# Attention, a greedy router and eight experts in one kernel: the router's and the experts' instructions put in order by one list scheduler, and the second pieces of the weights computed on VectorE

## The chip, the cores and the metric

The kernel runs on one core of a Trainium2 chip. The core has TensorE (PE, matrix products into the accumulator memory PSUM), VectorE (DVE), ScalarE (ACT), GpSimd (POOL), SyncE (SP) and DMA queues. Each engine works through its own queue in order, and the engines wait for each other by semaphores. The metric is the device time of one execution in microseconds (us).

## What is computed

Causal attention with a bias over 8 batches, 8 heads, 576 positions and 64 channels gives 4608 tokens of 512 channels. A router assigns the tokens to 8 experts, and each expert is a two-layer network:

```python
attn = softmax(where(causal, scale * q @ k.T + min(bias, 0), -1e9))
x = (attn @ v).transpose(0, 2, 1, 3).reshape(4608, 512)
logits = x @ w_gate                                # 8 experts
for idx in argsort(-logits.flatten()):             # greedy, from the largest logit on
    tok, e = idx // 8, idx % 8
    if assigned[tok] < 0 and counts[e] < 576:      # 576 places in each expert
        assigned[tok] = e; counts[e] += 1
for e in range(8):
    m = assigned == e
    out[m] = maximum(x[m] @ w1[e], 0) @ w2[e]      # 512 -> 1024 -> 512
```

## The kernel before

**Pieces.** Products are made of 16-bit pieces: an operand is split into a first piece (rounded to f16) and a second one (the remainder), and three of the four products of pieces are summed in PSUM. So every weight of an expert is loaded in f32 into a buffer `wst` and split. An expert has 12 loads: 4 of `w1` (128x1024, 512 KB) and 8 of `w2` (128x512, 256 KB), gathered by an indirect DMA on GpSimd's queue (L1012), since the router decides which expert comes next.

**The split before.** `Moe.weights` makes the first piece on ScalarE (L1017). For most loads ScalarE then scales the buffer in place (L1019) and GpSimd subtracts (L1027). For some loads of `w1` (three of expert 0's, the third of the others') one VectorE instruction over 1024 columns does both (L1025).

**The attention** comes first and keeps an order of its own. Only its comments differ between the two kernels.

**The router** (`Router`) fills one expert per phase, eight phases. A phase looks for the threshold at which some expert's remaining places are used up: seven steps, one digit each. In a step VectorE compares all keys with 32 digits (`ge`, L820), TensorE counts (L834), VectorE copies (`ca`, L838), TensorE sums (L844), VectorE compares with the places left (`pe`, L846), TensorE spreads this (L851), and VectorE takes the digit (`jc`, L854), subtracts (`wd`, L857) and goes on. Each link waits for the one before. `choose` (L773 to L788) prepares a phase; the update of the unassigned tokens (L921 to L937) ends it. `places` (L944 to L980) turns the chosen tokens into ids: one-hot matrices `ob`, `rv`, `ol` on VectorE, 40 small products on TensorE (`pi`, L973, in two groups of 20), then `ids`.

**The experts.** With the ids of an expert GpSimd gathers its tokens (`xg`, L1042), five tiles of 128 (the last of 64). SyncE transposes them by DMA into `xT`; for expert 0 TensorE does (L1052). The first layer is 8 groups of 12 pairs of products (512 columns in L1075, 64 in L1076), each followed by a ReLU on ScalarE (L1080) and a remainder on VectorE (L1089). The second layer is 112 products of 512 columns (L1109, L1100); ScalarE scales the result and GpSimd scatters it (L1121).

**The order.** `Clock` holds a rough time for each engine. A loop walks through the products of expert after expert, and after each product lets the search, the places and the loads go on when their time by a table (`AFTER`, `PACE`, `LAT` and others) has come, the router at most two phases ahead. Constant products (`warm`, L1251: 10, 16 and 12 of them) stand in the wait before expert 0.

Of the kernel before, what the change touches and what calls it, by code (L numbers as in the profile page):

```python
# [18 lines left out]
S = 576  # L19
# [7 lines left out]
QS = 32.0                 # scale of the q and k pieces  # L27
YS = 8.0 * QS * QS        # scale of the exponents in PSUM
# [22 lines left out]
class Attention:  # L51
# [23 lines left out]
    # ---- constants  # L75
# [27 lines left out]
    def gate(self):  # L103
        """The gate's pieces."""
# [85 lines left out]
    def prep_units(self, g):  # L190
        """Pieces of q, k, v. Pass 1 is [q hi; aux] . [k hi; aux], pass 2 is [q hi; q lo] . [k lo; k hi]."""
# [63 lines left out]
    def q0(self, par, i):  # L255
        """Where query tile i of a head lies: an odd head's last 64 queries come first."""
# [74 lines left out]
    def st_units(self, g):  # L331
        """S^T, exp, remainder of one group; returns units."""
# [145 lines left out]
    def tail(self, g, pr):  # L478
        """The last batch, two heads at a time, with transposes on the tensor engine: a list of units."""
# [71 lines left out]
    def run(self):  # L551
# [10 lines left out]
        def later(n0, units):  # L562
            """A list of (step, unit), made when step n0 comes."""
# [93 lines left out]
WARM = (10, 16, (2, 2, 2, 2, 4))  # L657
YSC = 1.0 / (VS * WS1 * WS2)
# what the order of the instructions goes by (us)
RLATE = 0.3  # L660
SLATE = -1.0
PACE = 1.7
GPACE = 1.8
PLEAD = 0.7
LAT = 3.3
HOP = -0.6
AHEAD = 0.5
DV0 = (0, 1, 2)
DV = (2,)
EARLY = 4  # L670
EARLY2 = 1
WARM = (10, 16, (2, 2, 2, 2, 4))
YSC = 1.0 / (VS * WS1 * WS2)
MARGIN = (0.0, 0.2)
# [8 lines left out]
class Router:  # L683
# [73 lines left out]
    def psum(self, shape, dt=F32):  # L757
        return self.ps.tile(shape, dt, name="psr")
# [601 lines left out]
```

## Time and profile before

| | |
|---|---|
| device time, median of 3 runs (lowest to highest) | 919.23 us (917.11 to 926.0) |
| span of the profiled execution | 923.2 us |
| TensorE busy, share of the span | 811.1 us, 88% |
| weight loads on TensorE | 484.3 us, 52% |
| VectorE | 656.4 us, 71% |
| GpSimd | 550.6 us, 60% |
| ScalarE | 460.6 us, 50% |
| read from and written to the chip's memory | 72.49 and 19.49 MB |

A span is the time from the first to the last instruction of the profiled execution; it lies 4.0 us above the median of the runs. A busy share is an average over very different stages: attention fills the first 399 us, the search for the first expert some 44 more, and the rest belongs to experts and router together. TensorE is the busiest engine, but its busy time holds products at a reduced clock too. Rows of the trace give a start and a length in us, the engine, the line of the kernel, the operation, the output and the inputs, and in brackets how long the engine had been idle before and what it waited for.

### The profile page before, as it was taken

Reading aid. Unit: us, or ns where it says so; the run is one execution under the profiler, and the core shown is the slowest. Engines: PE = TensorE matmul, PEld = TensorE weight load, DVE = VectorE, ACT = ScalarE, POOL = GpSimd, SP = SyncE. Lnnn points to the kernel's source line nnn. Section 1 sums busy time; section 2 is a strip of 40 time slices with the busy share of each in tenths; the row PEclk is TensorE's granted clock in tenths of the full one; section 3 lists DMA queues with packets and bytes.
Section 4 is the critical chain, followed back from the end, with each engine's and each line's share of the span. In section 5 each row is a group of like instructions: output and inputs, shape, how many; then the busy total and the mean of one; then the engine's idle time right before and its main releaser. Section 6 shows DMA issues by size and latency. Waiting matters only on the chain.

```text
span 923.2 us, 22391 instructions
## 1 busy us (share of the span) xinstructions
PE 811.1 (88%) x8719; PEld 484.3 (52%) x8719; DVE 656.4 (71%) x2077; ACT 460.6 (50%) x952; POOL 550.6 (60%) x582
## 2 busy tenths in 40 slices
PE   2889999989998999946998769989899989899996
PEld 0456676757676777723543334444444545444442
DVE  6895898989898987877887496896868874413010
ACT  5465676667775767713541352543524343526411
POOL 5544565656674677605646666686766675767601
PEclk9995798979897999966998799999999999999999
DMA  7763685978876772414324536446484537547201
GB/s 191 230 162 110 173 201 138 184 190 207 195 212 170 185 186 45 111 53 143 82 102 122 113 126 139 156 104 151 138 132 151 133 118 178 122 123 178 91 13 40
DMA packets 118400, 129.17 MB, mean 140 GB/s; under 512 B 79889, under 2 KB 80405, under 8 KB 118294
## 3 DMA queue, kind: packets, MB, share of 16 engines
q1 hardware_dynamic: 100114, 74.81, 34.6%
q0 software_dynamic: 15744, 52.46, 19.1%
q8 instruction: 68, 1.11, 0.5%
q10 hardware_dynamic: 2436, 0.48, 0.3%
q14 instruction: 38, 0.31, 0.1%
HBM read 72.49 MB, written 19.49 MB: 100 GB/s over the span
## 4 chain that ended last, share of the span: by engine, by line
PE 47%; DVE 23%; issue 11%; POOL 8%; DMA 7%; ACT 2%; SPq 0%; POOLq 0%; ACTq 0%; DVEq 0%
PE py L1109 9%; PE ph L1075 6%; PE po L408 5%; PE pst L339 5%; PE pst L341 4%; PE pss L275 4%; DMA wst<-in_w_dram,iw 3%; PE po L410 3%; PE po L409 3%; DVE scr L269 2%; DVE ge L820 2%; POOL wst L1012 2%; PE pst L344 2%; PE pss L288 2%; POOL xg L1042 2%
## 5 line engine op out<-in xcount | busy, mean ns | idle before, releaser
L351 POOL TENSOR_TENSOR R<-P 128x512 f16<-128x512 f32 x158 | 179.6, 1144 | 119.5 <-ACT P L349 57.0
L1075 PE MATMUL ph<-xT,w1p 128*128 128x512 f16 x768 | 205.3, 392 | 4.2 <-DMA xT<-xg 4.2
L1109 PE MATMUL py<-w2p,hT 128*128 128x512 f16 x768 | 180.4, 386 | 0.0
L349 ACT ACTIVATE P<-pst 128x512 f32<-128x512 f32 (+1 forms) x224 | 122.5, 553 | 98.8 <-PE pst L344 67.3
L1076 PE MATMUL pht<-xT,w1p 128*128 128x64 f16 x768 | 150.4, 196 | 1.9 <-DMA xT<-xg 1.9
L269 DVE CUSTOM_DVE_ANT_0 scr<-pss,mS 128x512 bf16<-128x512 f32 (+3 forms) x256 | 120.5, 482 | 32.3 <-PE pss L275 21.9
L1012 POOL DMA_INDIRECT wst<-in_w_dram,iw x96 | 98.8, 1030 | 66.0 <-issue 26.6
L408 PE MATMUL po<-V,P 128*128 128x65 f16 (+1 forms) x960 | 136.1, 206 | 0.1
L410 PE MATMUL po<-V,R 128*128 128x65 f16 (+1 forms) x960 | 134.0, 202 | 2.2 <-DVE R L351 2.2
L339 PE MATMUL pst<-Q,K 70*128 70x384 f16 (+4 forms) x576 | 133.3, 265 | 2.4 <-ACT P L349 2.4
L409 PE MATMUL po<-Vl,P 128*128 128x64 f16 (+1 forms) x960 | 134.0, 201 | 0.0
L341 PE MATMUL pst<-Q,K 128*128 128x384 f16 (+4 forms) x576 | 132.1, 262 | 0.0
L1075 PEld LDWEIGHTS <-w1p 128*128 128x128 f16 x768 | 76.7, 100 | 96.1 <-issue 17.0
L1109 PEld LDWEIGHTS <-hT 128*128 128x128 f16 x768 | 70.5, 99 | 80.0 <-issue 5.5
L408 PEld LDWEIGHTS <-P 128*128 128x128 bf16 (+1 forms) x960 | 95.2, 103 | 22.5 <-issue 9.5
L409 PEld LDWEIGHTS <-P 128*128 128x128 bf16 (+1 forms) x960 | 97.3, 106 | 5.1 <-issue 3.0
L410 PEld LDWEIGHTS <-R 128*128 128x128 f16 (+1 forms) x960 | 97.6, 104 | 2.3 <-DVE R L351 2.3
L275 PE MATMUL pss<-K,Q 67*128 67x512 f16 (+3 forms) x256 | 78.3, 342 | 21.5 <-DMA K<-pk 13.0
L1080 ACT ACTIVATE hT<-ph 128x512 f16<-128x512 f32 x64 | 37.8, 592 | 112.8 <-PE ph L1075 85.8
L1027 POOL TENSOR_TENSOR w2p<-wst,w2p 128x512 f16<-128x512 f32 x64 | 75.9, 1190 | 26.2 <-ACT wst L1019 25.4
L1121 POOL DMA_INDIRECT out_dram<-y,ids x40 | 41.7, 1043 | 71.5 <-ACT y L1111 58.7
L1089 DVE SCALAR_TENSOR_TENSOR hT<-ph,hT 128x512 f16<-128x512 f32 x64 | 43.8, 686 | 53.0 <-ACT hT L1080 52.9
(215 smaller groups left out, 1683.3 us busy)
## 6 DMA issues: line engine op xcount, KB each, us to landing
rq<-in_q_dram SPq DMA_DIRECT2D x32, 288.0 KB
rk<-in_k_dram SPq DMA_DIRECT2D x32, 288.0 KB
rv<-in_v_dram SPq DMA_DIRECT2D x32, 288.0 KB
Q<-Q SPq DMA_DIRECT2D x62, 144.0 KB
K<-K SPq DMA_DIRECT2D x62, 144.0 KB
xs<-xp SPq DMA_DIRECT2D x32, 256.0 KB
wst<-in_w_dram,iw POOLq DMA_INDIRECT x96, 4.1
xs<-xp SPq DMA_DIRECT2D x8, 128.0 KB
```

The lines of the kernel that those rows point to most:

```text
L269: nc.vector.tensor_tensor_reduce(scr[:, :n], ps, mask, 1.0, init, OP.add, OP.max, o)
L339: nc.tensor.matmul(ps[o, c0:c0 + n], K[0:70, 0, par, pr, ks], Q[0:70, 0, par, pr, q0:q0 + n], start=True, stop=False)
L341: nc.tensor.matmul(ps[o, c0:c0 + n], K[:, 1, par, pr, ks], Q[:, 1, par, pr, q0:q0 + n], start=False, stop=not diag)
L349: nc.scalar.activation(P[:, c0:c0 + n], ps[:, :n], AF.Exp, scale=1.0 / YS)
L351: self.post(lambda: eng.tensor_tensor(R[:, c0:c0 + n], P[:, c0:c0 + n], strided_hi(P)[:, c0:c0 + n], op=OP.subtract), T["RT"][0 if gp else 1])
L408: nc.tensor.matmul(po[:n, i, :], H[rows, c:c + n], V[rows, pr, sl, :], start=f, stop=False)
L409: nc.tensor.matmul(po[:n, i, 0:64], H[rows, c:c + n], Vl[rows, pr, sl, :], start=False, stop=False)
L410: nc.tensor.matmul(po[:n, i, :], R[rows, c:c + n], V[rows, pr, sl, :], start=False, stop=l)
L1012: nc.gpsimd.indirect_dma_start(out=t[:, :n], out_offset=None, in_=src, in_offset=bass.IndirectOffsetOnAxis(ap=iw[:, k:k + 1], axis=0))
L1075: nc.tensor.matmul(ph, w, xT[:, 0:4, 4 * b + c], start=first, stop=last)
L1076: nc.tensor.matmul(pt[:, f], w, xT[:, 4, 4 * b + c, 0:64], start=first, stop=last)
L1109: nc.tensor.matmul(py, hT[:, f, a, 128 * i:128 * i + n], w2p[:, f, b], start=first, stop=last)
```

## The change

Search, places, loads, splits, gathers and products all become tasks of one graph (`Plan`). A task has an engine, a duration, the tasks it depends on, a priority and the buffers that it takes or uses; buffers come from rings with a fixed number of tiles. The list scheduler keeps a time for each engine and starts, again and again, the task that can start first; among those of an engine that are ready it takes the one of the best priority (router 0, remainders of the ReLU and gathers 1, an expert's loads, splits and products 2 + its number). A low task can be held back by 0.35 or 0.4 us if a better one comes soon. Router products have a `slack` of 0, 0.15 or 0.3 us (phase 0, 1, later). A load is taken to land 2.6 us after 1 us of issue and its share of a common 180 KB/us. The order in which tasks are started is the order of the instructions.

With it: every second piece of a weight is made by VectorE, in parts of 512 columns (L1221), two for a `w1` load; the scaling in place on ScalarE and the subtraction on GpSimd are gone. There are 5 `wst` buffers, not 4. Marking who reached a threshold (`jm`, `t`, `run`) is done once for six steps and once for the last, not in every step. The 40 place products form one group. The first three groups of expert 0's first layer come tile by tile, 128 columns each, as the tiles arrive. There are 16 constant products. Loads of `w2` of experts 0 and 1 wait for the ids.

```diff
+class Plan:
+    HOP = 0.04
+    KBUS = 180.0
...
+    def add(self, e, dur, f, deps=(), prio=1, takes=(), uses=(), lat=None, hold=0.0, kb=0, slack=0.0):
...
+        if e == "t":
+            x.occ, x.lat = dur, dur + 0.19
+        else:
+            x.occ = max(dur - dict(v=0.08, a=0.11, p=0.04, s=0.0)[e], 0.03)
+            x.lat = dur + self.HOP
...
+    def run(self):
+        while self.count:
+            best = None
+            for e, w in self.wait.items():
...
+                for t, x in sorted(c, key=lambda z: (z[1].prio, z[1].rank)):
+                    if t <= t0 + 1e-9:
+                        pick = (t, x)
+                        break
+                t, x = pick
+                if x.hold:
+                    soon = [z for z in c if z[1].prio < x.prio and z[0] < t + x.hold]
...
+            t, x = best
+            self.start(t, x)
...
+        x.at = t
+        if x.kb:
+            self.dma = max(self.dma, t + 1.0) + x.kb / self.KBUS
+            x.lat += self.dma - t
+        x.end = t + x.lat
+        self.free[x.e] = t + x.occ
...
-                yield AFTER["ca"]
-                pb = self.psum([128, E])
+                T(0.28, f_pa, takes=[A], uses=[ge])
+                V(0.19, lambda ca=ca, A=A, n=n: v.tensor_copy(
+                    ca.t[:4 * n], A.t[:4 * n, 0:32].rearrange("p (c e) -> p c e", c=4)), takes=[ca], uses=[A])
...
-            def hi():
-                t = box[0]
-                nc.scalar.activation(dst[:, 0], t[:, :n], AF.Copy, scale=sc)
-                if not ve:
-                    nc.scalar.activation(t[:, :n], t[:, :n], AF.Copy, scale=sc)
-                return n / 1200 * (1 if ve else 2)
-
-            def lo():
-                t = box[0]
-                if ve:
-                    nc.vector.scalar_tensor_tensor(dst[:, 1], t[:, :n], sc, dst[:, 0], op0=OP.mult, op1=OP.subtract)
-                    return "v", n / 900
-                nc.gpsimd.tensor_sub(dst[:, 1], t[:, :n], dst[:, 0])
-                return "p", n / 480
+            ld = pl.add("p", 1.0, lambda: nc.gpsimd.indirect_dma_start(
+                out=st.t[:, :n], out_offset=None, in_=src,
+                in_offset=bass.IndirectOffsetOnAxis(ap=iw.t[:, k:k + 1], axis=0)), [tw] + ([ti] if k >= 4 and j < 2 else []), prio=prio, takes=[st], uses=[iw],
+                lat=self.LAND, kb=n / 2)
+            first = key == 0
+            hi = pl.add("a", 1.05 if n == FF else 0.63, lambda: nc.scalar.activation(
+                dst.t[:, key, 0], st.t[:, :n], AF.Copy, scale=sc), [ld], prio=prio,
+                takes=[dst] if first else (), uses=[st] + ([] if first else [dst]), hold=0.4)
+            lo = [pl.add("v", 0.7, lambda c=c: nc.vector.scalar_tensor_tensor(
+                dst.t[:, key, 1, c:c + 512], st.t[:, c:c + 512], sc, dst.t[:, key, 0, c:c + 512], op0=OP.mult,
+                op1=OP.subtract), [hi], prio=prio, uses=[st, dst], hold=0.35) for c in range(0, n, 512)]
...
+    pl = Plan()
+    last = behind = None
+    for j in range(E):
+        info = {}
+        last = R.phase(pl, j, info, last, 0)
+        first = info if j == 0 else first
+        behind = M.expert(pl, j, info, behind, R.ident16 if j == 0 else None)
...
+    for n in range(16):
+        x = pl.add("t", 0.43, warm, [x], prio=1.5, uses=[hot])
+    pl.run()
```

What this does to the queues is seen at three places. In the tables a row is one instruction: line, operation, output<-inputs, size.

VectorE inside a router step, while an expert's products run. Before:

```order
L838 CAST ca<-psr 128x32
L861 TENSOR_SCALAR jm<-jc 128x1
L862 SCALAR_TENSOR_TENSOR t_10860<-psr,jm,Ws 128x8
L846 TENSOR_TENSOR pe<-psr,rem 128x8
L864 TENSOR_TENSOR run<-run,t_10860 128x8
L854 TENSOR_REDUCE jc<-psr 128x1
L857 TENSOR_SCALAR wd<-y,jc 128x40
L820 TENSOR_TENSOR ge<-wd,kj 128x1280
```

VectorE inside such a step in the changed kernel (`w1p` is the split weight):

```order
L1002 CAST ca_8801<-psa 128x32
L1221 SCALAR_TENSOR_TENSOR w1p_8859<-wst_8867,w1p_8859 128x512
L1010 TENSOR_TENSOR pe_8803<-psb,rem 128x8
L1221 SCALAR_TENSOR_TENSOR w1p_8859<-wst_8867,w1p_8859 128x512
L1015 TENSOR_REDUCE jc_8808<-psb 128x1
L1019 TENSOR_SCALAR wd_8806<-y_8799,jc_8808 128x40
L975 TENSOR_TENSOR ge_8798<-wd_8806,kj 128x1280
L986 SCALAR_TENSOR_TENSOR y_8800<-wd_8806,dg 128x40
L1221 SCALAR_TENSOR_TENSOR w1p_8859<-wst_8863,w1p_8859 128x512
```

The marking has left the step, and parts of second pieces stand where VectorE waits for TensorE's counts and sums.

GpSimd at the end of an expert, with the next one's loads and gathers. Before:

```order
L1012 DMA wst<-in_w_dram,iw 128x1024 x4
L1027 TENSOR_TENSOR w1p<-wst,w1p 128x1024
L1012 DMA wst<-in_w_dram,iw 128x512
L1027 TENSOR_TENSOR w1p<-wst,w1p 128x1024
L1012 DMA wst<-in_w_dram,iw 128x512
L1027 TENSOR_TENSOR w1p<-wst,w1p 128x1024
L1027 TENSOR_TENSOR w2p<-wst,w2p 128x512
L1012 DMA wst<-in_w_dram,iw 128x512
L1042 DMA xg<-xs,ids 128x1024
```

GpSimd at a like place in the changed kernel:

```order
L1213 DMA wst_8867<-in_w_dram,iw_8831 128x1024
L1213 DMA wst_8863<-in_w_dram,iw_8831 128x1024
L1213 DMA wst_8864<-in_w_dram,iw_8831 128x1024
L1187 DMA xg_8868<-xs,ids_8840 128x1024 x4
L1187 DMA xg_8868<-xs,ids_8840 64x1024
L1213 DMA wst_8865<-in_w_dram,iw_8831 128x1024
L1213 DMA wst_8866<-in_w_dram,iw_8831 128x512
L1213 DMA wst_8867<-in_w_dram,iw_8831 128x512
L1302 MEMSET spacer 1x1
L1303 DMA out_dram<-y_8875,ids_8839 4608x512
```

GpSimd's queue holds only the issue of transfers now, and the five gathers follow each other.

VectorE after the first search, on the way to expert 0's ids. Before:

```order
L944 SCALAR_TENSOR_TENSOR Z<-Y,X 128x80
L946 SCALAR_TENSOR_TENSOR si<-Z 128x40
L948 TENSOR_SCALAR d<-si 128x40
L949 TENSOR_SCALAR d<-si 128x40
L951 CAST db<-d 128x80
L958 TENSOR_TENSOR ob<-i_468,db 128x720
L961 TENSOR_TENSOR rv<-ob,rb 128x720
```

The same place in the changed kernel:

```order
L1119 SCALAR_TENSOR_TENSOR Z_8842<-Y_8835,X_8832 128x80
L1085 TENSOR_TENSOR tm_8819<-oh,gg_8813 128x320
L1120 SCALAR_TENSOR_TENSOR si_8843<-Z_8842 128x40
L1090 TENSOR_REDUCE cp_8820<-tm_8819 128x8
L1121 TENSOR_SCALAR d_8844<-si_8843 128x40
L1094 TENSOR_SCALAR sel_8822<-W,vstar_8826 128x8
L1122 TENSOR_SCALAR d_8844<-si_8843 128x40
L1095 TENSOR_TENSOR gv_8815<-gg_8813,U 128x40
L1123 CAST db_8845<-d_8844 128x80
L1096 TENSOR_SCALAR sel_8822<-sel_8822 128x8
L1127 TENSOR_TENSOR ob_8846<-i_468,db_8845 128x720
```

The update of the unassigned tokens (`tm`, `cp`, `sel` and what follows) has moved from behind the ids to between the steps that lead to them.

More of the change, by code (lines that the diff above doesn't have):

```diff
@@ L678, with __init__, slot @@
 NEG = -1.0e30
+SLACK = (0.0, 0.15, 0.3)
 NONE = 1.0e9
 NT = 8 * S
+class Buf:
+    __slots__ = ("ring", "t", "users")
+    def __init__(self, ring):
+        self.ring, self.t, self.users = ring, None, []
+class Ring:
+    def __init__(self, tiles):
+        self.slots = [[t, None] for t in tiles]
+    def slot(self):
+        best = None
+        for s in self.slots:
+            if s[1] is None:
+                at = 0.0
+            elif all(u.at is not None for u in s[1].users):
+                at = max(u.end for u in s[1].users)
+            else:
+                continue
+            if best is None or at < best[0]:
+                best = (at, s)
+        return best
@@ L985 @@
+        info["ids"] = (chain[0], ids)
 class Moe:
+    LAND = 2.6
     def __init__(self, tc, ctx, xs, w1, w2, out):
@@ new lines, in expert, with scatter, go @@
+        w2n = {(f, b): [W2[f][0]] if b == 0 else W2[f][1] for f in range(8) for b in range(2)}
+        def scatter(i, n, dep):
+            def go():
+                nc.gpsimd.memset(self.spacer, 0.0)
+                st = nc.gpsimd.indirect_dma_start(
+                    out=self.out, out_offset=bass.IndirectOffsetOnAxis(ap=ids.t[:n, i:i + 1], axis=0),
+                    in_=y.t[:n, i], in_offset=None)
+                for s in self.scat:
+                    self.tc.declare_no_dep(st.ins, s.ins, reason="other rows")
+                self.scat.append(st)
+            pl.add("p", 1.1, go, [dep], prio=2, uses=[y, ids], lat=3.0, kb=2 * n)
@@ L1170, in route_and_experts @@
+        return closing
 def route_and_experts(tc, ctx, R, xs, w1, w2, out):
     R.pools(ctx)
+    R.rings()
     M = Moe(tc, ctx, xs, w1, w2, out)
-    info = {j: {} for j in range(E + 1)}
-    clock = Clock()
-    now = dict(j=0, out=0)
-    def search():
-        for j in range(E):
-            yield from R.phase(j, lambda k, t, j=j: info[j].update({k: t}))
-    def places():
-        for j in range(E):
-            while "places" not in info[j]:
-                yield None
-            yield from R.places(j, *info[j]["places"], lambda k, t, j=j: info[j].update({k: t}))
@@ L1188, in route_and_experts @@
-    streams = [dict(g=g, next=0.0, ready=0.0, pe=0.0) for g in (search(), places())]
-    def step(s, force=False):
-        if clock.t < s["next"] and not force:
-            return False
-        clock.at["t"] = max(clock.t, s["ready"]) + s["pe"]
-        s.update(ready=0.0, pe=0.0)
-        x = next(s["g"], None)
-        if x is None:
-            return False
-        done = clock.use("v", x[0])
-        if x[1] is None:
-            s["next"] = done - AHEAD
-        else:
-            lead = sum("ids" in info[i] for i in range(E)) - now["j"]
-            s.update(next=done + x[1] + MARGIN[min(lead, 2) - 1], ready=done + HOP, pe=x[2])
-        return True
@@ L1208, in load @@
-    def load(j, k):
-        u = info[j]["wu"][k]
-        def hi():
-            clock.after("a", u[1](), 0.1, lo)
-        def lo():
-            clock.use(*u[2]())
-            now["out"] -= 1
-            info[j]["left"].discard(k)
-        u[0]()
-        now["out"] += 1
-        clock.after("p", 1.04, LAT, hi)
-    def fetch(j, force=False):
-        d = info[j]
-        if "weights" in d and "w1p" not in d:
-            d["w1p"], d["w2p"], d["wu"] = M.weights(d["weights"], dve=DV)
-            d["left"], d["next"] = set(range(12)), 0
-        if "ids" in d and "xT" not in d:
-            d["xT"], d["xu"] = M.gather(d["ids"])
-        if d.get("xu"):
-            clock.use("p", 1.04)
-            d["xu"].pop(0)()
-            return GPACE
-        if "wu" in d and d["next"] < 12 and (now["out"] < 4 or force):
-            while now["out"] >= 4:
-                clock.wait()
-            load(j, d["next"])
-            d["next"] += 1
-            return PACE
-        return None
@@ L1244, in route_and_experts @@
-    hot = []
-    def warm(n):
-        for _ in range(n):
-            if not hot:
-                hot.append(R.ps.tile([128, 512], F32, name="warm", tag="psr"))
-            tc.nc.tensor.matmul(hot[0], R.ones, R.qb.rearrange("p c n -> p (c n)"), start=True, stop=True)
-    d = info[0]
-    while "weights" not in d:
-        step(streams[0], True)
-    d["w1p"], d["w2p"], d["wu"] = M.weights(d["weights"], dve=DV0)
-    d["left"], d["next"] = set(range(4, 12)), 4
-    for u in d["wu"][:4]:
-        u[0]()
```

794 lines of the change are left out of this document (424 added, 370 removed).

## The prediction

> **What bounds the kernel now.** I first read the span and then the busy times by stretch, from the experts' first product (442.8, its row stands with the pace below) to their last (915.2): this stretch, the end behind it, the part in which the router still works, and a piece of that.
>
> ```profile
> span 923.2 us, 22391 instructions
> ...
> 442.80:915.20 472.40, 431.20 (x3361) 215.21 (x3356) 282.35 (x821) 190.05 (x289) 292.70 (x295) 0.96 0.47 121
> 915.20:923.20 8.00, 0.00 (x0) 0.00 (x0) 0.00 (x0) 0.48 (x1) 0.97 (x1) 0.71 0.08 33
> ...
> 442.80:800.00 357.20, 316.15 (x2647) 160.02 (x2643) 264.28 (x794) 148.48 (x224) 235.32 (x229) 0.94 0.51 130
> ...
> 680.00:740.00 60.00, 58.71 (x520) 30.39 (x519) 46.77 (x159) 23.11 (x36) 38.39 (x38) 1.00 0.67 148
> ```
>
> The numbers in a row are stretch, length, then busy us of PE, weight load, VectorE (DVE), ScalarE (ACT), GpSimd (POOL), and the granted clock. The expert stretch is bound by TensorE, which idles 472.4 - 431.2 = 41.2 us and runs at 0.96 of its clock; 0.04 x 472.4 = 18.9 us more go to that. So about 60 us could be had, and 431.2 - 18.9 = 412 us is the work. The pace of the products says the same:
>
> ```profile
> 442.78 0.38 PE L1075 MATMUL ph<-xT,w1p 128*128 128x512 f16 x1
> ...
> 540.50 0.38 PE L1075 MATMUL ph<-xT,w1p 128*128 128x512 f16 x1
> ...
> 544.66 0.38 PE L1075 MATMUL ph<-xT,w1p 128*128 128x512 f16 x1
> ...
> 909.70 5.34 PE L1109 MATMUL py<-w2p,hT 128*128 128x512 f16 x24
> ```
>
> From 540.50 to 544.66 seventeen steps of 0.245 us lie between the starts of the first layer's pairs, and 24 products of the second take (5.34 - 0.38) / 23 = 0.216 each. An expert has 96 pairs and 112 products: 96 x 0.245 + 112 x 0.216 = 47.7 us, eight of them 381.5. The other 30 us are the router's products, some 4.4 per expert: an expert needs 52 us of TensorE. I take 411 us for the whole.
>
> Then I asked which TensorE groups had waited, in the expert stretch (last part of a row: idle us before, and what ended it):
>
> ```profile
> L1075 PE MATMUL ph<-xT,w1p 128*128 128x512 f16 x768 | 205.3, 392 | 4.2 <-DMA xT<-xg 4.2
> L1076 PE MATMUL pht<-xT,w1p 128*128 128x64 f16 x768 | 150.4, 196 | 1.9 <-DMA xT<-xg 1.9
> L834 PE MATMUL psr<-oh,ge 128*128 128x32 f16 (+1 forms) x416 | 17.1, 177 | 9.9 <-DVE ge L820 9.8
> L973 PE MATMUL pi<-rv,ol 128*32 128x36 bf16 x280 | 12.4, 202 | 21.5 <-DVE ol L968 21.5
> L844 PE MATMUL psr<-ca,qb 128*128 128x8 f16 (+1 forms) x168 | 10.4, 167 | 2.7 <-DVE jm L861 2.7
> ```
>
> Of 41.2 us idle, 9.9 + 21.5 + 2.7 = 34.1 are router products that stand in TensorE's queue before VectorE has their operands; only 6.1 are a late transfer. Why VectorE is late, the chain of waits and GpSimd's timeline show for the longest of these waits:
>
> ```profile
> 541.47 2.33 DVE rv L961
> ...
> 544.11 2.71 DVE sel L929
> ...
> 547.58 3.77 DVE U L934
> ...
> 551.88 0.90 PE pi L973 x20
> ...
> 541.25 2.14 POOL L1027 TENSOR_TENSOR w1p<-wst,w1p 128x1024 f16<-128x1024 f32 x1
> ...
> 544.65 2.13 POOL L1027 TENSOR_TENSOR w1p<-wst,w1p 128x1024 f16<-128x1024 f32 x1
> ...
> 548.04 2.13 POOL L1027 TENSOR_TENSOR w1p<-wst,w1p 128x1024 f16<-128x1024 f32 x1
> 550.12 1.16 POOL L1027 TENSOR_TENSOR w2p<-wst,w2p 128x512 f16<-128x512 f32 x1
> ...
> L934 DVE TENSOR_TENSOR U<-U,X x7: 193/195/3842, 435.2 to 768.0; 128x40 f32<-128x40 f32 x7
> ...
> L934 DVE TENSOR_TENSOR U<-U,X 128x40 f32<-128x40 f32 x6 | 8.7, 1448 | 0.0
> ...
> 552.71 0.61 PE L1075 MATMUL ph<-xT,w1p 128*128 128x512 f16 x1
> ...
> 553.18 0.61 PE L1075 MATMUL ph<-xT,w1p 128*128 128x512 f16 x1
> ```
>
> Each long VectorE instruction ends when a GpSimd subtraction ends (543.8, 546.8, 551.3). The update of U takes 0.195 us at the median and 3.84 at worst (min/median/max in ns), and 1.448 on average over the experts' stretch; the chain that TensorE waits for was blocked three times in 10 us. Behind the wait pairs start 0.47 apart in place of 0.245: the clock is down.
>
> **The change part by part.** First, the second pieces leave GpSimd and ScalarE for VectorE.
>
> ```profile
> L1027 POOL TENSOR_TENSOR w2p<-wst,w2p 128x512 f16<-128x512 f32 x64 | 75.9, 1190 | 26.2 <-ACT wst L1019 25.4
> L1027 POOL TENSOR_TENSOR w1p<-wst,w1p 128x1024 f16<-128x1024 f32 x21 | 45.4, 2162 | 17.6 <-ACT wst L1019 17.4
> ...
> L1019 ACT ACTIVATE wst<-wst 128x512 f32<-128x512 f32 (+1 forms) x85 | 62.5, 735 | 7.5 <-ACT w2p L1017 0.4
> ...
> L1025 DVE SCALAR_TENSOR_TENSOR w1p<-wst,w1p 128x1024 f16<-128x1024 f32 x7 | 16.6, 2378 | 2.5 <-ACT w1p L1017 2.5
> ...
> L1025 DVE SCALAR_TENSOR_TENSOR w1p<-wst,w1p x10: 1211/1226/3742, 428.5 to 841.2; 128x1024 f16<-128x1024 f32 x10
> ...
> L1089 DVE SCALAR_TENSOR_TENSOR hT<-ph,hT 128x512 f16<-128x512 f32 x64 | 43.8, 686 | 53.0 <-ACT hT L1080 52.9
> ```
>
> GpSimd loses 121 us, ScalarE 62.5; neither bounds anything, so this alone is worth nothing. VectorE gets 8 x 16 = 128 parts of 512. One costs between half of 1.226 and the 0.686 of a like instruction on 512: I take 0.68, together 87 us, and 10 x 1.23 = 12 go. What it loses is the blocking. Its lower end is two groups alone: L934, 6 x (1.448 - 0.195), and L1025, 7 x (2.378 - 1.226), some 16 us. Its upper end is all of GpSimd's 121. If the two engines met by chance, VectorE being busy 282 of 472 us, 0.6 x 121 = 72 us; I take 70, since the chain above shows nearly every meeting as a block. Over six router phases that is 11.7 us less and (87 x 6 / 8 - 8.6) / 6 = 9.4 us more (8.6 are the seven L1025 of this stretch) per phase. VectorE idles 357.2 - 264.3 = 93 us up to 800, 15 per phase, and the order shown ahead puts the parts between the router's instructions. I take half of them as hidden in that idle time.
>
> How long is a phase? The place products mark it:
>
> ```profile
> 492.73 0.85 PE L973 MATMUL pi<-rv,ol 128*32 128x36 bf16 x20 [4.42 <-DVE ol L968]
> ...
> 610.84 0.90 PE L973 MATMUL pi<-rv,ol 128*32 128x36 bf16 x20 [3.31 <-DVE ol L968]
> ...
> 715.83 0.89 PE L973 MATMUL pi<-rv,ol 128*32 128x36 bf16 x20
> ```
>
> With 551.88 the phases last 59.2, 59.0 and 105.0 us (the last two together), on average 55.8. Now 55.8 - 11.7 + 4.7 = 48.8, under the 52 us that TensorE needs: TensorE, no longer the router, sets the pace, and the router gets ahead.
>
> Second, the order. A list scheduler places each instruction where its durations let it start, with 0.15 or 0.3 us to spare before a router product. So a wait is planned away, unless an operand is late; what is then left I read from 680 to 740, where the old order fits: 1.3 of 60 us idle. 2 to 3% of the 300 us with a router are 6 to 9: I take 8. Ends: 0, and the 34 of now. All 40 places of the tokens come in one group of products, not two; the TensorE time is the same. The gathers stand together on GpSimd, no scatter between them; expert 1's, the 6.1 us of late transfer, are asked for when a shorter phase is over, so I count this wait as gone.
>
> Third, the head up to the first product. The rows:
>
> ```profile
> 428.78 1.82 POOL L1042 DMA_INDIRECT xg<-xs,ids  x1 [1.59 <-DVE ids L980]
> ...
> 435.64 0.92 POOL L1042 DMA_INDIRECT xg<-xs,ids  x1 [0.30 <-issue]
> ...
> 433.16 0.48 DVE L921 TENSOR_TENSOR tm<-oh,gg 128x320 f32<-128x320 f16 x1
> ...
> 436.20 2.87 DVE L775 TENSOR_TENSOR eq<-L,m 128x320 f32<-128x320 f32 x1
> ```
>
> The update of the unassigned tokens, 433.16 to 436.20, now stands between the steps that lead to the first ids, which delays the gathers by up to 3.0 us. On the other side the search of phase 1 starts sooner, and products on single 128-token tiles start before the last tile is there. Between 440 and 446 I leave the effective start at 443. The 16 constant products instead of 38 that hold the clock up lie in the same wait. The tail stays 8.0 us: same last steps.
>
> One rule speaks against the change. The first gather's issue takes 1.82 us while L1025 runs, the last, alone, 0.92. The Trainium skill's page "SBUF — State Buffer", section "SBUF: two separate sides", says that a DMA issued from GpSimd is starved of descriptors while a VectorE instruction holds the shared port pair; the trace agrees, 0.9 us more. By that rule in full, each of five gathers waits for a whole part, 5 x 0.68 = 3.4 us, and the time would be 869 in place of 866; by the rows it is 0.9 at most, within the head's bounds.
>
> The sum: 443 + 411 + 8 + 8.0 = 870 us of span, 53 less than 923.2. That execution's span is 4.0 above the median of the runs, 919.2; I take the same 53 from the median: **866 us**.
>
> **The rivals.** Late landings. First pieces on ScalarE wait for weights; behind them stand, in order, the ReLUs, and on VectorE the second pieces ahead of router steps, so TensorE is held too.
>
> ```profile
> DMA to landing us min/median/max: 3.2/4.1/9.8
> ```
>
> The scheduler allows 2.6 + 1 + KB / 180, 6.4 us for the large and 5.0 for the small pieces. The median speaks for it, the maximum against it: 3.4 to 4.8 us late. One such wait per expert, less the slack, and slow products behind it is some 4 us, 7 x 4 = 28 more: 894 less the 8 already counted, **886 us**.
>
> VectorE as the bound. If only the lower end of the blocking goes (16 / 6 = 2.7 per phase) and no part is hidden, a phase is 55.8 - 2.7 + 9.4 = 62.5 us; TensorE waits 10.5 in each, 63 in all, and the clock falls behind each wait, some 2 us by the slow pairs above: 443 + 411 + 63 + 12 + 8 = 937 of span, **933 us**, not faster than before. It decides from a phase of about 60 us. The 15 us of idle VectorE per phase and 541 to 551 speak against it. In between, with 70 us of blocking gone but TensorE held by mistimed parts a third of a microsecond at each of 21 router groups in six phases, 42 us, stands **908 us**.
>
> **How the numbers follow.** The forecast 0.62 (its own range 854 to 878, from the head's 440 to 446 and 0 to 15 us of waits), late landings 0.22, mistimed parts 0.08, VectorE as the bound 0.06, and 0.02 for something faster than all. A range of 853 to 896 leaves out the last three and a part of the second, about 0.2. A change of 1% is what a measurement of this kernel tells from none: the three runs span 917.1 to 926.0. Faster by over 1% (under 910): 0.91; within: 0.05; slower: 0.04.
>
> **What would show it.** Right: no VectorE instruction over twice its median in the expert stretch; 128 second pieces near 0.68 us; TensorE idle there under 12 us, and its clock at 0.99; place products without a wait; first product between 438 and 444. Wrong: ScalarE's first pieces waiting for transfers with TensorE idle behind router groups at the same time (late landings); place products still over 55 us apart (VectorE).

## The result and the profile after

The changed kernel takes 871.1 us (median of 4 runs, 863.33 to 874.49) against 918.17 us for the kernel before, run beside it (4 runs, 912.17 to 926.0). The ratio is 0.948, with a 95% interval from 0.941 to 0.955. The forecast was 866 us.

The profiled execution of the changed kernel took 870.18 us. First the stretches of its trace, with the same columns as ahead: from the first product of the experts to the last product, the end, and three stretches of a little over one expert each, the first three, to which the text comes back below.

```profile
core 0 of [0], span 868.5 us
...
439.28:860.50 421.22, 415.84 (x3467) 216.60 (x3466) 270.65 (x839) 130.75 (x208) 177.61 (x207) 1.00 0.53 138
860.50:868.50 8.00, 0.00 (x0) 0.00 (x0) 0.00 (x0) 0.00 (x0) 0.98 (x1) 0.75 0.08 33
439.28:495.40 56.12, 55.62 (x629) 34.27 (x629) 47.01 (x155) 20.60 (x31) 30.01 (x32) 1.00 0.60 166
495.40:549.80 54.40, 53.74 (x483) 28.00 (x482) 45.40 (x158) 18.48 (x30) 25.11 (x29) 1.00 0.58 151
549.80:608.50 58.70, 55.98 (x496) 29.00 (x495) 48.05 (x166) 18.84 (x29) 24.85 (x29) 0.97 0.67 145
```

The stretch of the experts is 421.2 us long, where it was 472.4. TensorE idles 421.22 - 415.84 = 5.4 us in it, where it idled 41.2, and its granted clock is 1.00, where it was 0.96. These two things are the gain of this stretch: 35.8 us are idle time, and the other 15.4 are busy time, for which the clock is enough: by the sum ahead 0.96 had cost 18.9 us, so some 3.5 us of other work have come in. Next the groups of TensorE's router products in this stretch, with the idle time ahead of them at the end of the row, and then the groups of VectorE that carried the argument (shortest, median and longest in ns in the rows that name a stretch of starts):

```profile
L998 PE MATMUL psa<-oh,ge 128*128 128x32 f16 (+1 forms) x410 | 16.7, 177 | 4.6 <-DVE ge L975 4.6
L1141 PE MATMUL psc<-rv,ol 128*32 128x36 bf16 x280 | 11.3, 203 | 0.9 <-DVE ol L1133 0.9
L1007 PE MATMUL psb<-ca,qb 128*128 128x8 f16 (+1 forms) x164 | 10.1, 167 | 0.0
```

```profile
L1221 DVE SCALAR_TENSOR_TENSOR w1p<-wst,w1p x64: 670/682/694, 434.5 to 781.4; 128x512 f16<-128x512 f32 x64
L1221 DVE SCALAR_TENSOR_TENSOR w2p<-wst,w2p x64: 669/684/754, 444.6 to 791.0; 128x512 f16<-128x512 f32 x64
L1100 DVE TENSOR_TENSOR U<-U,X x7: 192/193/195, 427.3 to 689.2; 128x40 f32<-128x40 f32 x7
```

The place products had waited 21.5 us and now wait 0.9. The update of U, which once took 3.84 us, never takes more than 0.195. Added over all VectorE instructions from the first product of the experts on, the time above the shortest instruction of the same line and operands (where it is more than 0.1 us) is 69.3 us in the trace before, 68.1 of it beside a GpSimd subtraction, and 2.5 us in the trace after.

### The profile page after: what moved, and what is told of

Read it like the earlier page. It is cut to its first block, busy times and chain, and to the rows that moved or that the text cites. A ratio compares the mean times of both kernels' runs of the same rounds, so it can differ in the third digit from the quotient of the medians.

```text
span 868.5 us, 22418 instructions
## 1 busy us (share of the span) xinstructions
PE 784.9 (90%) x8805; PEld 479.8 (55%) x8805; DVE 642.8 (74%) x2090; ACT 395.7 (46%) x866; POOL 430.1 (50%) x489
## 4 chain that ended last, share of the span: by engine, by line
PE 64%; DVE 16%; issue 9%; DMA 6%; POOL 2%; ACT 1%; SPq 1%; POOLq 0%; DVEq 0%
PE psm L1249 16%; PE psm L1323 14%; PE po L408 5%; PE pst L339 4%; PE pst L341 4%; PE pss L275 3%; DVE scr L269 3%; PE po L410 3%; PE po L409 3%; PE psm L1320 2%; PE psn L1253 2%; PE pst L344 2%; DVE mp L308 2%; PE psa L998 2%; PE pss L288 1%
## 5 line engine op out<-in xcount | busy, mean ns | idle before, releaser
L1249 PE MATMUL psm<-xT,w1p 128*128 128x512 f16 (+1 forms) x876 | 195.1, 353 | 0.5 <-ACT xT L1204 0.5
L1323 PE MATMUL psm<-w2p,hT 128*128 128x512 f16 x768 | 175.9, 381 | 0.0
L1253 PE MATMUL psn<-xT,w1p 128*128 128x64 f16 x768 | 142.1, 192 | 0.0
L1249 PEld LDWEIGHTS <-w1p 128*128 128x128 f16 x876 | 79.6, 98 | 80.0 <-issue 0.6
L1269 ACT ACTIVATE hT<-psm 128x512 f16<-128x512 f32 x64 | 38.2, 597 | 126.1 <-PE psm L1249 107.8
L1271 DVE SCALAR_TENSOR_TENSOR hT<-psm,hT 128x512 f16<-128x512 f32 x64 | 44.1, 689 | 46.5 <-ACT hT L1269 46.1
L1334 ACT ACTIVATE y<-psm 128x512 f32<-128x512 f32 x32 | 19.1, 597 | 121.8 <-PE psm L1323 121.8
```

The source lines that it names most:

```text
L1249: nc.tensor.matmul(ps[:, tiles[0]:tiles[-1] + 1] if len(tiles) > 1 else ps[:, tiles[0]], lhs(f, c, a), xT.t[:, tiles[0]:tiles[-1] + 1, 4 * ...
L1253: nc.tensor.matmul(pt.t[:, 64 * f:64 * f + 64], lhs(f, c, a), xT.t[:, 4, 4 * b + c, 0:64], start=s, stop=e)
L1323: nc.tensor.matmul(py.t, hT.t[:, f, a, 128 * i:128 * i + 128], w2p.t[:, f, b], start=f == 0 and k == 0, stop=f == 7 and k == 2)
```

## The experiments

They ran on three chips, called the second, third and fourth here. The kernel before takes 948.93, 942.12 and 947.29 us on them, not 918, so each run is read by its ratio to the kernel before on the same chip. No chip is noted for the first result; that it was another one is taken from these times and from the waits told next.

### The changed kernel again

On the third chip it ran unaltered, and on the fourth.

> The changed kernel itself, unaltered, as the measure for the runs beside it on the same chip: 0.948 of the time before by the first measurement. On the chip of the first four experiments, where before took 949 in place of 918, VectorE and ScalarE had waits of 2 to 6 us behind which the trace shows no other engine; if these belong to the chip and not to the edits, they are here too where before is again near 949, and absent where it is near 918.

> The changed kernel, unaltered, beside the next two on the same chip: 0.945 to 0.955 where the waits without a cause are absent, 0.96 to 0.975 where they are present.

Measured: 914.47 us, ratio 0.971 (0.964 to 0.978), and 909.69 us, ratio 0.961 (0.954 to 0.968). The change is faster on each chip, but by less than on the first. The reason lies in waits that the first chip does not show, in either kernel. The view of VectorE's waits (total us, times, longest) of the run on the third chip:

```profile
DVE ca L1002 <- remote: 17.7, 4, 7.2
DVE pe L1010 <- remote: 5.3, 2, 2.8
DVE jc L1015 <- remote: 4.7, 2, 3.8
```

"remote" and "issue" mean that the trace shows nothing that ends the wait: the products that these instructions read had long been done. Each stands between two router products, so TensorE waits with it. To size this, I took every idle time of TensorE over 0.1 us in the experts' stretch. It counts as such a wait where its own row says "issue", or where over half of it, or more than 0.8 us, lies inside a wait of over 0.8 us on VectorE or ScalarE that ends with "issue" or "remote". On the third chip that is 30.8 of 36.7 us of idle time; 6.0 us stand behind VectorE's work.

The kernel before was traced on the fourth chip.

> The kernel before, unaltered, for its trace on a chip other than the first. The changed kernel stood at 0.948 of it on the first chip and at 0.971 on the third, where 30.8 of TensorE's 36.7 us of idle time stood behind waits of VectorE, ScalarE or TensorE itself that no other engine ends in the trace. Theory: before has such waits too, but fewer of them cost time, since TensorE waits for the router anyway: under 20 us on such a chip, and the ratio differs by the rest, some 2%. Rival: before has as many (25 to 35 us), and the ratio differs for another reason. On a chip like the first: none, ratio 1.

Measured: 946.82 us, ratio 1.001, as it must be. Of its 60.3 us of idle time only 14.7 are such waits (10.9 + 3.8), and 45.6 stand behind VectorE's work. The changed kernel has 30.8 on the third chip and, in the run told next, 32.7 on the fourth. The difference of some 16 to 18 us, 1.7 to 1.9% of 947, stands against ratios that are 0.023 and 0.013 higher than the first, each difference known to about 0.01. So the theory agrees in size, as far as the intervals go; what makes the waits is not settled (last section).

### The first places ahead of the update

```
-        self.places(pl, info, X, Y, placed, 0 if j < 2 else prio)
+        self.places(pl, info, X, Y, placed, -1 if j == 0 else prio)
```

> The changed kernel with one number changed: in the first phase the steps to the places (and ids) come ahead of the update of the unassigned tokens, which stood between them. Theory: the update's instructions between 423.58 and 428.28 (3.0 us of work) delay the ids, the gathers and the first product; without that the ids are there near 428.7 in place of 431.7, the first product near 436.5 in place of 439.3, and the time falls by 2 to 3 us, to 868. Rival: the second pieces of the first expert's weights or phase 1's search, now 3 us later, are what the first expert waits for next; the first product comes sooner but TensorE then waits: no change, 870 to 872.

> The kernel with the places of the first phase ahead of the update, now beside the changed kernel on one chip. Theory: the first product 2.3 to 3 us after which the experts follow unchanged: 0.003 less in the ratio than the run before this. Rival: nothing, since phase 1's search comes later by as much and expert 1 waits for it: the same ratio within 0.002.

Measured: 906.98 us on the second chip, ratio 0.955 (0.950 to 0.960), and 912.0 on the fourth, ratio 0.965 (0.959 to 0.971), beside 0.961 for the changed kernel. The edit moves nothing: on every engine the order of the instructions is that of the changed kernel. The planner takes whatever can start first, and a priority only decides among what can start at the same moment. A step of a chain on VectorE is ready 0.04 us after the end of the one ahead, while the planner has the engine free 0.08 us before that end, so in this gap an instruction of the other chain slips in, whatever its priority. So both runs are repeats of the changed kernel, and give its ratio on the second chip; neither the theory nor its rival was tested. Whether the places would come sooner without the update between them was not tried.

### The new order without the move of the second pieces

```
-            lo = [pl.add("v", 0.7, ... , [hi], prio=prio, uses=[st, dst], hold=0.35) for c in range(0, n, 512)]
+            if k == 2 or (j == 0 and k < 3):
+                lo = [pl.add("v", 1.23, ... whole piece ... )]
+            else:
+                s2 = pl.add("a", 1.05 if n == FF else 0.63, lambda: nc.scalar.activation(st.t[:, :n], ... scale=sc), [hi], ...)
+                lo = [pl.add("p", 2.12 if n == FF else 1.15, lambda: nc.gpsimd.tensor_sub(...), [s2], ...)]
```

> The changed kernel's list scheduler, but the second pieces are made as before the change: ScalarE scales in place, GpSimd subtracts whole pieces, VectorE takes only w1's third piece of each expert (and the first three of expert 0). The planner knows these times (1.05, 0.63 on ScalarE; 2.12, 1.15 on GpSimd) but no blocking. Theory A (what was taken away is the mutual blocking of VectorE and GpSimd; the order alone is worth little): the update of U and the other two-operand VectorE instructions are again up to 3.8 us long, VectorE's excess is again about 70 us, TensorE idles 30 us or more in the expert stretch, and the time is 900 to 925. Theory B (the planned order is the gain, and which engine subtracts matters little, since VectorE had idle time): long instructions may come back, but TensorE idles under 12 us and the time is 868 to 880.

Measured: 950.15 us, ratio 1.004 (1.000 to 1.008), beside 0.955 for the changed kernel on the same chip. The stretch of its experts, the groups of its router products with their waits, and one group of VectorE:

```profile
426.00:936.50 510.50, 446.27 (x3472) 225.31 (x3471) 266.80 (x724) 189.50 (x293) 295.75 (x293) 0.94 0.43 113
```

```profile
L998 PE MATMUL psa<-oh,ge 128*128 128x32 f16 (+1 forms) x400 | 16.5, 178 | 17.2 <-DVE ge L975 16.9
L1141 PE MATMUL psc<-rv,ol 128*32 128x36 bf16 x280 | 11.7, 203 | 12.2 <-DVE ol L1133 11.3 <-issue 0.8
L1007 PE MATMUL psb<-ca,qb 128*128 128x8 f16 (+1 forms) x164 | 10.1, 167 | 17.4 <-DVE ca L1002 15.6 <-issue 1.6
```

```profile
L1019 DVE TENSOR_SCALAR wd<-y,jc 128x40 bf16<-128x40 f32 x35 | 26.9, 768 | 1.2
```

TensorE waits 43.4 us for VectorE outside the waits without a cause, nearly the 45.6 of the kernel before. VectorE's time above the shortest is 61.4 us, 59.9 of it beside a GpSimd subtraction. A planned order with blocked instructions in it is worth nothing here. Theory A holds, theory B falls.

### GpSimd made busy again, in two ways

Both runs add instructions on GpSimd to the changed kernel, one behind each first piece that had such a partner before, on a tile that nobody reads.

```
+            if k != 2 and (j or k > 2):
+                pl.add("p", 2.12 if n == FF else 1.15, lambda: nc.gpsimd.tensor_sub(
+                    self.dc[:, :n], self.da[:, :n], self.db[:, :n]), [hi], prio=prio)
```

```
+                pl.add("p", 2.12 if n == FF else 1.15, lambda: nc.gpsimd.memset(self.da[:, :2 * n], 0.0), [hi], prio=prio)
```

> The changed kernel, with GpSimd given back the subtractions that it lost (21 of 128x1024 and 64 of 128x512, on a tile of its own that nobody reads; the planner knows their 2.12 and 1.15 us). The output is the reference's; nothing but GpSimd's time is added, 118 us. Theory A (two engines that both read two operands block each other): VectorE's two-operand instructions are stretched again up to 3.8 us, its excess is 50 to 70 us, TensorE idles 30 us more, ratio to before 0.98 to 1.01 in place of 0.948. Rival (GpSimd's queue, not a block: the loads, gathers and scatters stand behind the subtractions): VectorE's durations stay at their medians and the time goes up by late transfers alone, and then it goes up as much with the memsets of the next run.

> As the run before it, at the same places of GpSimd's queue and with the same planned times, but memsets (128x2048 and 128x1024, near 2.05 and 1.03 us at the 0.52 of a 128x512) in place of the subtractions: GpSimd is as busy within 10%, but reads no operand. Theory A: VectorE's two-operand instructions keep their medians, ratio 0.945 to 0.965. Rival (queue): ratio as in the run with the subtractions.

Measured: 956.87 us with the subtractions, ratio 1.011 (1.002 to 1.021), and 916.24 with the memsets, ratio 0.974 (0.966 to 0.981), beside 0.971 for the changed kernel on the same chip. The groups of GpSimd and of VectorE, first with the subtractions, then with the memsets, then of the changed kernel on this chip:

```profile
L1231 POOL TENSOR_TENSOR dc<-da,db 128x512 f16<-128x512 f32 x64 | 80.9, 1263 | 3.1
L1231 POOL TENSOR_TENSOR dc<-da,db 128x1024 f16<-128x1024 f32 x21 | 45.3, 2157 | 0.6
...
L1227 DVE SCALAR_TENSOR_TENSOR w2p<-wst,w2p 128x512 f16<-128x512 f32 x64 | 54.3, 858 | 19.7 <-ACT w2p L1224 15.6 <-issue 4.0
L1019 DVE TENSOR_SCALAR wd<-y,jc 128x40 bf16<-128x40 f32 x35 | 24.8, 708 | 1.1
```

```profile
L1226 POOL MEMSET da<- 128x1024 f32 x64 | 61.7, 963 | 1.8
L1226 POOL MEMSET da<- 128x2048 f32 x22 | 40.2, 1829 | 0.2
...
L1222 DVE SCALAR_TENSOR_TENSOR w2p<-wst,w2p 128x512 f16<-128x512 f32 x64 | 42.9, 683 | 19.0 <-ACT w2p L1219 14.0 <-issue 5.0
L1019 DVE TENSOR_SCALAR wd<-y,jc 128x40 bf16<-128x40 f32 x35 | 19.8, 567 | 1.1
```

```profile
L1221 DVE SCALAR_TENSOR_TENSOR w2p<-wst,w2p 128x512 f16<-128x512 f32 x64 | 43.2, 684 | 20.8 <-ACT w2p L1218 16.9 <-ACT y L1334 3.9
L1019 DVE TENSOR_SCALAR wd<-y,jc 128x40 bf16<-128x40 f32 x35 | 9.3, 264 | 1.2
```

In both runs the order on TensorE, VectorE and ScalarE is the same, instruction for instruction, so only what GpSimd does sets them apart. (It is not quite the order of the changed kernel, since the planner counts the added work.) The subtractions fill GpSimd for 126.2 us and cost 42 us of time, more than the 28 that the change brings on this chip and a little more than the ratio of 0.98 to 1.01 that theory A expected. The memsets fill it for 101.9 us at the same places of its queue and cost 2, less than the runs can tell. So GpSimd's queue is not the cost. ScalarE's scaling was not put back either, so the loss does not need it.

What differs is what VectorE suffers: the second pieces, which read two operands, take 0.858 us beside subtractions and 0.683 beside memsets, as alone. The one-operand L1019, 0.264 us on average alone, takes 0.708 and 0.567: a memset, which reads nothing, stretches it too. VectorE's time above the shortest is 85.8 us with subtractions, 42.1 with memsets and 2.0 without either. The Trainium skill's page "SBUF — State Buffer", section "Who interferes with whom", says just this: a VectorE instruction with two inputs in the on-chip memory contends with a GpSimd instruction that reads there, not with one that only writes, while copies and one-operand instructions of the fast modes contend with either. The traces agree, with the numbers above, for the two-operand pieces; for L1019 they show only that both stretch it, not in which mode it runs.

That 42.1 us of stretch cost nothing and 85.8 cost 42 us is not proportional. TensorE's waits for VectorE are 6.0 us without, 18.3 with memsets and 34.1 with subtractions; but with memsets TensorE's idle time is 37.2 us in all and without them 36.7, while the waits without a cause fall from 30.8 us to 18.9. So on this chip these waits may hide a part, and what the memsets would cost on the first chip is not known. How the 42 us divide into idle time and clock cannot be read from this trace either: its execution (964.87 us) was granted a clock of 0.84 on average, 0.82 in the attention, where nothing was added, while the four others had 0.90 to 0.93.

### The move of the second pieces without the new order

First with the old rules, which count VectorE's new work:

```
-DV0 = (0, 1, 2)
-DV = (2,)
+DV0 = tuple(range(12))
+DV = tuple(range(12))
```

> The kernel before with one thing changed: all twelve pieces of every expert have their second piece made on VectorE in one instruction each (1024 or 512 wide), none on GpSimd and no scaling on ScalarE. The old order (streams, due times) stays. Theory A (blocking): no VectorE instruction over twice its median, phases near 50 us in place of 55.8, TensorE's 41 us of idle time fall to about 20 where the old order's due times still miss, time 885 to 900. Theory B (order): the old order goes on missing its due times, all the more with 1.2 us pieces in VectorE's queue; idle time stays 35 to 50 us and the time is 910 to 930. VectorE as the bound (a rival of the prediction) would show here as phases of 60 us or more.

Measured: 956.5 us, ratio 0.999 (0.993 to 1.005). Its first-layer products and VectorE's update of U:

```profile
L1075 PE MATMUL ph<-xT,w1p 128*128 128x512 f16 x768 | 210.7, 392 | 48.8 <-DMA xT<-xg 44.6 <-issue 3.0 <-ACT xT L1053 1.2
...
L934 DVE TENSOR_TENSOR U<-U,X 128x40 f32<-128x40 f32 x6 | 1.1, 188 | 0.0
```

The blocks are gone (U at 188 ns), and the gain is gone too, to a wait that neither theory had named: 44.6 us for the tokens of the next expert. The old rules, told of 12 pieces on VectorE, put the place products late: in this trace they end at 481.9, 550.7, 617.5 and 683.4, and the next experts start at 503.6, 570.4, 639.8 and 707.1, 20 to 24 us later each time, while the expert at work ends 7 to 11 us before that. Ids, five gathers and five transposes fill the time between.

So the next run keeps TensorE's order exactly as before, by telling the old rules nothing. Only the second pieces change their engine, and ScalarE's scaling goes:

```
-                if not ve:
-                    nc.scalar.activation(t[:, :n], t[:, :n], AF.Copy, scale=sc)
...
-                nc.gpsimd.tensor_sub(dst[:, 1], t[:, :n], dst[:, 0])
+                nc.vector.scalar_tensor_tensor(dst[:, 1], t[:, :n], sc, dst[:, 0], op0=OP.mult, op1=OP.subtract)
                 return "p", n / 480
```

> The kernel before, with its planner told nothing: the order on TensorE is word for word that of before, and only the engine of the second pieces changes (VectorE in one instruction each, at the place where GpSimd's stood; ScalarE's scaling goes). In the earlier run with the old rules the planner charged VectorE for the pieces and moved the places of the tokens to 11 us of products ahead of an expert's end, while ids, gathers and transposes take some 22: TensorE then waited 46 us for the tokens. Theory A1 (blocking is most of it; that loss came from the moved places): VectorE waits of 34 us fall under 15, late tokens cost 5 to 20 (14 us of products stand behind the places here), ratio 0.965 to 0.985. Theory A2 (blocking and order are worth something only together: with the blocks gone the old order leaves too little time for the tokens in any case): TensorE's waits for tokens rise to 30 us or more, ratio 0.99 to 1.01.

> The order of before with all second pieces on VectorE, beside the changed kernel on one chip: what is left between the two is the worth of the new order (list scheduler, halves of 512, early places, finer first products). From the third chip: TensorE idle behind VectorE and late tokens 13 us here and 6 there, so 7 us or 0.008 more in the ratio than the changed kernel where the waits without a cause are equal. Rival (the order is worth half of the gain, which those waits hid on the third chip): 0.02 or more.

Measured: 917.12 us on the third chip, ratio 0.974 (0.968 to 0.981), beside 0.971 for the changed kernel; 921.04 on the fourth, ratio 0.972 (0.965 to 0.979), beside 0.961. The stretch of the experts and the products that wait most, of the first of the two:

```profile
436.00:907.20 471.20, 433.53 (x3355) 214.85 (x3354) 276.04 (x905) 128.65 (x205) 170.35 (x208) 0.96 0.47 120
```

```profile
L1073 PE MATMUL ph<-xT,w1p 128*128 128x512 f16 x768 | 205.5, 390 | 11.5 <-issue 6.0 <-DMA xT<-xg 5.1 <-ACT xT L1051 0.3
L851 PE MATMUL psr<-pe,quart 128*128 128x8 f16 x42 | 7.1, 170 | 11.0 <-DVE pe L846 10.0 <-issue 0.8
```

Of 36.9 us of idle time, 23.8 are waits without a cause, 7.8 stand behind VectorE's work (45.6 in the kernel before on the fourth chip) and 5.1 behind late tokens. Theory A1 holds: with the order untouched the move alone takes the waits for VectorE away. What is left for the new order, with the halves, the fifth buffer, the moved marking and the finer first products in it, is 0.003 on one chip and 0.011 on the other, with intervals that overlap. The rival that gave the order half of the gain (0.02 or more) is outside on the third chip; on the fourth each difference is known to about 0.01, so it is unlikely there but not shut out. On the first chip, where no waits without a cause hide a part, the two were not run side by side.

### Whole pieces of 1024 in place of halves

```
-            lo = [pl.add("v", 0.7, lambda c=c: ... c:c + 512 ... hold=0.35) for c in range(0, n, 512)]
+            lo = [pl.add("v", 1.23 if n == FF else 0.7, lambda c=c: ... c:c + n ... hold=0.35) for c in range(0, n, n)]
```

> The changed kernel with the second pieces of w1 made in one instruction of 1024 in place of two of 512 (planned at 1.23 us). Theory: the halves matter because a router step that becomes ready behind a piece waits for its rest; 32 pieces now hold VectorE 0.55 us longer at a time, and each of the 28 in the expert stretch can delay a router group: 0 to 8 us more, likeliest 873 to 876. Rival: the planner orders around it and VectorE does 0.14 us less per piece (4.4 us in all, off the path): 870, no difference that can be measured.

Measured: 915.01 us, ratio 0.962 (0.956 to 0.969), beside 0.955 (0.950 to 0.960) for the changed kernel on that chip. The difference of 8 us in the medians (906.98 for the changed kernel's order) points the way of the theory; the intervals overlap, so it is not settled. By the rule above TensorE's waits for VectorE are 6.0 us here and 4.5 there, so only 1.5 of the 8 us show as such waits in the two traces. A whole piece takes 1.219 us, two halves 2 x 0.684 = 1.37.

## Why the prediction was right, step by step

**The sum.** Forecast and measured, in us of the profiled execution: head 443 and 439.3; work 411 and 415.8; waits 8 and 5.4; end 8.0 and 8.0; together 870 and 868.5. The three errors are small, and that they nearly cancel is luck. Most of the 4.8 us of work lies in two of the stretches shown: TensorE is busy 55.6 us with the first expert, which now takes 629 products and not some 480, and 56.0 us in the third, at a clock of 0.97, where 53.7 do in the second. So a part of what the head gains is paid in the first expert. The step from the span to the median was the weak one: I took 53 us from the median, because the span was to shrink by 53. But the profiled execution of the kernel before was its slowest run (926.0), and that of the changed kernel lies below its median (870.18 and 871.1). The spans differ by 54.7 us and the medians by 47.1, which is 5.9 less than the 53; the median of before, taken again beside the change, was 1.1 lower, and the rest is the 5 us between 866 and 871. By the bounds that it names, 3 us of head either way and 0 to 15 us of waits, the forecast's own range would be 855 to 876, not 854 to 878.

**The blocking.** I took 70 us between ends of 16 and 121; the traces give 69.3, of which 2.5 stay. The parts take 0.682 and 0.684 us where 0.68 was said. The experiment with subtractions, beside the one with memsets, shows that it is the blocking and not GpSimd's time or queue that costs. The three ends read as ends of a subtraction are not all that: the first subtraction ends at 541.25 + 2.14 = 543.39, 0.4 us ahead of 543.8, and U, from 547.58 to 551.35, stood beside two subtractions in a row. One sign of being right is not met to the letter: L899 and L1121 take 0.43 and 0.36 us at most, over twice their medians of 0.18.

**The phase.** A phase was reckoned at 48.8 us, under the 52 that TensorE needs. It came out shorter still, and was the wrong test. The place products of the changed kernel:

```profile
L1141 PE MATMUL psc<-rv,ol x320: 192/204/216, 427.9 to 707.8; 128*32 128x36 bf16 x160
```

These are eight groups of 40, the first at 427.9 and the eighth at 706.4. The eighth follows the seventh (690.8) after 15.7 us; the six steps ahead of that are (690.8 - 427.9) / 6 = 43.8 us each. But the router had been ahead in the kernel before too: its last place products ended at 801.9, 65 us ahead of the expert that they serve (867.2). With the added subtractions the first seven groups are 60 us apart, and the fifth and the sixth expert start 72 and 85 us behind the end of theirs (662.9 and 735.3, 721.7 and 806.5); TensorE waits all the same. Being ahead does not help a product that stands at a fixed place of TensorE's queue: it waits if its operand is late at that place. So the condition of the rival "VectorE as the bound", a phase of 60 us, is not what decides either.

**The order.** Here the credit was wrong. The step "so a wait is planned away" made the list scheduler the reason why 34 us of waits would shrink to 8. With the new order and the blocks, TensorE waits 43.4 us for VectorE; with the old order and no blocks, 7.8 and 8.8. The waits were the blocks' work, and they go with them. The size came out right because both parts of the change were made together, which is luck as far as this step goes.

**The transfers.** Late landings were given 0.22, with one wait per expert. ScalarE does wait for weights again and again, twice for 3.7 us, but one such wait in all reaches TensorE, early in the third expert's second layer: ScalarE waits for the next expert's weights, their second piece stands on VectorE ahead of a router step, and TensorE follows.

```profile
581.16 1.06 ACT L1218 ACTIVATE w1p<-wst 128x1024 f16<-128x1024 f32 x1 [3.70 <-DMA wst<-in_w_dram,iw]
582.25 0.69 DVE L1221 SCALAR_TENSOR_TENSOR w1p<-wst,w1p 128x512 f16<-128x512 f32 x1 [3.40 <-ACT w1p L1218]
582.86 0.16 DVE L1015 TENSOR_REDUCE jc<-psb 128x1 f32<-128x8 f32 x1
...
584.21 0.41 PE L998 MATMUL psa<-oh,ge 128*128 128x32 f16 x10 [2.72 <-DVE ge L975]
```

That is the chain as the rival told it, and its price of some 4 us is right: 2.72 us here, and with the clock behind it the stretch from 549.8 to 608.5 is 4.3 us longer than the one ahead of it. Only it happens once, not seven times. Mistimed parts (0.08) did not come either: TensorE's other waits for VectorE in the stretch are three, 2.0 us together. The late tokens of expert 1 (6.1 us) are gone, as forecast. On the other side, the old rules lost their whole gain to late tokens in one run (44.6 us), and 5.1 us were left in the run with TensorE's order untouched; the prediction had no rival of this kind.

**The head.** The update of the unassigned tokens does stand between the steps to the ids:

```profile
423.58 0.48 DVE L1085 TENSOR_TENSOR tm<-oh,gg 128x320 f32<-128x320 f16 x1
...
431.52 0.16 DVE L1148 SCALAR_TENSOR_TENSOR ids<-pf 32x4 int32<-32x4 f32 x1
...
431.95 1.18 POOL L1187 DMA_INDIRECT xg<-xs,ids  x1 [4.07 <-DVE dg L897]
...
438.18 1.09 POOL L1187 DMA_INDIRECT xg<-xs,ids  x1 [0.31 <-issue]
...
439.30 0.77 PE L1249 MATMUL psm<-xT,w1p 128*128 128x128 f16 x11 [0.55 <-ACT xT L1204]
```

The first gather is asked for at 431.95, 3.2 us later than before (3.0 were said). Yet the first product comes 3.5 us sooner, because it needs only the first 128 tokens: 7.4 us from the first gather to it, where 14.0 had passed. The products on single tiles were worth more than I allowed by leaving 443 in place. Both readings rest on the traces alone; no run undid either.

The five gathers are issued in 6.2 us, where the rows of before have 6.9 between the first and the last. The section "SBUF: two separate sides" of the Trainium skill's page "SBUF — State Buffer" gives its rule for VectorE instructions in a two-port fast mode; the prediction took it over to two-operand pieces, and that these run in such a mode no trace shows. A whole VectorE part of delay for each gather, that rule in full, did not come.

## What to carry to other kernels

One engine can hold another up for longer than one of its own instructions lasts: here GpSimd's subtractions stretched VectorE's instructions with two operands, and L1019 with one as well. Look for a short instruction whose longest time ends where another engine's ends, and move or change one of the two before planning the order of the rest. A product that waits in an in-order queue is late at its own place, however far its chain is ahead. And when a planner is told of new work on an engine, check what it moves elsewhere: here it moved the request for the next expert's tokens and gave the gain back.

## What the runs showed of the hardware

The same program takes 871 us on one chip and 907 to 914 on three others. On those, VectorE and ScalarE stop for up to 10 us where the trace shows nothing left to wait for, and VectorE at nearly the same instructions in every run of the changed kernel: counted by the rows of the trace, at its instructions 1471, 1599, 1724, 1726, 1863, 1987 and 2127 on the second and third chip, five of the six distances between them being 124 to 140 long; the two traces of the fourth chip have six of the seven each. The list of DMA queues in the changed kernel's profile shows the instruction streams, by queue, kind, packets and MB:

```profile
q8 instruction: 69, 1.13, 0.5%
...
q14 instruction: 37, 0.30, 0.1%
```

A packet of q14 is 0.30 MB / 37, some 8 KB. The Trainium skill's page "Runtime: NRT & Kernel Launch", section "Instruction fetch mechanics", gives 64 bytes per instruction by its figures (16 KiB for 256) and calls the refill mostly hidden; 8 KB would then be, as an estimate from these figures, 128 instructions, near the distance of the stops. So late refills are a possible cause, which is argued and not shown: no run changed the instruction stream alone, no trace shows which queue feeds VectorE, and why the first chip has none of these waits is open.
